# The second attention moved into the first phase, V in token order, and whole rows in the mixing by U

## The chip, the cores and the metric

The kernel runs on one core of one Trainium2 chip. The metric is the device time of one execution in microseconds (us), the time of the slowest core, here the only one. A run is told from another by about 0.3% of the time, some 2.6 us.

## The reference

Eight batches of eight heads: 32 packed queries `p` attend to 576 keys and values of width 64, and then 576 queries `q` attend to the 32 packed results. The heads are laid side by side (512 columns), tokens are mixed by a product of rank 32, and a two-layer network of 512, 2048 and 512 columns follows. `U`, `V`, `w_ch1` and `w_ch2` come as 64-bit floats, the rest as 32-bit.

```python
def sm_attn(qq, kk, vv):
    s = scale * np.matmul(qq, kk.transpose(0, 1, 3, 2))
    a = np.exp(s - np.max(s, axis=-1, keepdims=True))
    a = a / (np.sum(a, axis=-1, keepdims=True) + 1e-09)
    return np.matmul(a, vv)
p_packed = sm_attn(p, k, v)                # 8 x 8 x 32 x 64
x = sm_attn(q, p_packed, p_packed)         # 8 x 8 x 576 x 64, then 8 x 576 x 512
h = x.transpose(0, 2, 1) @ U @ V           # U 576 x 32, V 32 x 576
u = x + h.transpose(0, 2, 1)
out = u + np.maximum(u @ w_ch1, 0.0) @ w_ch2
```

## The kernel before

**Two phases.** In the first phase a planner reorders what the code records: it makes one fixed order for each engine from a timeline of its own, and each engine then runs its list strictly in that order. From `tc.manual_schedule()` on the code's own order stands.

**First phase.** The attention of `p` runs in 16 units, two groups `g` of four heads for each of eight batches. A unit loads keys (`a_load`, tile `kx`) and values (`a_load_v`, tile `vt`, three buffers), transposes the keys (`a_turn`, `kT`), forms scores (`a_scores`, `s_ps`), exponentials (`a_softmax`), turns them back (`a_turn_back`), multiplies by the values (`a_pack`, `two`) and transposes the packed result (`a_heads`, `ppT`; parked in DRAM as `ppTd` for later batches). Beside it w1 (16 chunks) and the first tiles of w2 are converted from 64-bit floats: ScalarE takes an absolute value (L77 or L143), VectorE makes four passes (L78 to L81, `float32_of`), and for w2 ScalarE and GpSimd split the result into a high and a low float32r part (L158, L159).

**The attention of `q`** is a list of 24 steps for one batch, made by `attention(b, res)`: `load` (two tiles `x` of 576 KB), three `turn_q` for each group, `scores_q`, four softmax steps (the exponents `e` have one buffer; max, subtraction on GpSimd, exp, sum, product on GpSimd, and transposition into `aT`), three `tokens` steps (back to token order, `x` tiles for the high and low part), `mix1` (ten products with U, L304) and four `mix2` (products with V, L318 and L321). Since the 32 packed rows replace keys and values, nothing is multiplied out here: `ah`/`al` hold mixed attention weights, and `fold` (L361) multiplies w1 by the packed rows. In V's tile `vs` the columns stand as the reference has them (token 9i + c), and `mix2` picks them with a stride of nine floats, since the other tiles keep the tokens in blocks of equal c.

Steps are popped one after the other. The code pops the first attention three steps to a unit from unit 4 on, and records the load of the second at unit 13:

```python
        if i >= 4:
            for _ in range(3):
                if first:
                    first.pop(0)()
```

**Second phase.** Eight steps, one to a batch, of 16 column blocks `kt`: `gemm1` (twelve products with `ah`, `al` into the two `h_ps` banks, then ScalarE's relu `hh` and VectorE's rest `hl`, L599), `gemm2` of the block before (twelve products of 512 columns into `o`), and after every fourth block (2, 6, 10, 14) a `fold` for the blocks to come, whose rest `wtl` VectorE forms (L368). In the first step the remaining w2 tiles are loaded and converted too, one to a block, and the last units' `a_pack` and `a_heads` run in its blocks 0 to 3. The attention steps of batch b + 1 are popped between these products in step b: in the first step that is the second attention. `bank()` gives one of two PSUM banks, shared by turns, scores, tokens, mixing and folds.

Line numbers are those of the profile of the kernel before; in the changed kernel they are up to 13 higher from L165 on.

Of the kernel before, what the change touches and what calls it, by code (L numbers as in the profile page):

```python
# [8 lines left out]
F32 = mybir.dt.float32  # L9
# [10 lines left out]
def packed_attention_mixer_kernel(  # L20
# [141 lines left out]

    ua4 = const.tile([P, 5, 4, R], F32R, name="ua4")
    vs = const.tile([P, S], F32R, name="vs")

    def x_tile():
        return pipe.tile([P, 5 * 2 * P], F32, name="x", tag="x", bufs=2)
# [12 lines left out]
    def prepare_uv(ub, vbits):  # L180
        ux = float32_of(conv_tile(I32)[:, :5 * R], conv_tile(F32)[:, :5 * R], ub.rearrange("p (x t) -> p x t", t=2))
        for (n, ks) in ((P, slice(0, 4)), (64, slice(4, 5))):
            nk = ks.stop - ks.start
            src = ux.rearrange("p (k r) -> p k r", k=5)[:n, ks].unsqueeze(2).to_broadcast([n, nk, 4, R])
            nc.vector.tensor_copy(ua4[:n, ks], src)
            nc.vector.tensor_tensor(ua4[:n, ks, 1], src[:, :, 0], ua4[:n, ks, 0].bitcast(F32), op=ALU.subtract)
        vb = vbits.rearrange("p (x t) -> p x t", t=2)
        n = I // 2
        for hf in range(2):
            cs = slice(NT * n * hf, NT * n * hf + NT * n)  # L190
            vx = float32_of(conv_tile(I32)[:, :NT * n], conv_tile(F32)[:, :NT * n], vb[:, cs])
            nc.vector.tensor_copy(vs[:, cs], vx)
            nc.vector.tensor_tensor(vs[96:, cs], vx[96:], vs[96:, cs].bitcast(F32), op=ALU.subtract)


    def load_nat(x, src, b, g):
        nc.sync.dma_start(
            out=x.rearrange("p (h y) -> p h y", h=2),
            in_=src[b, 4 * g:4 * g + 4].rearrange("(h z) (i c) d -> (z i) h (c d)", z=2, c=NT))

    def turn(t, x, h, bank):

        x = x.rearrange("p (h y) -> p h y", h=2)
        t_ps = bank()
        if h < 2:
            for j in range(4):
                o = P * (2 * (j % 2) + j // 2)
                nc.tensor.transpose(t_ps[:, o:o + P], x[:, h, P * j:P * j + P], ident)  # L208
            src = t_ps.rearrange("p (k a z i) -> p a z k i", k=2, a=2, z=2)
            for a in range(2):  # L210
                dst = t[:, 2 * h:2 * h + 2, :4 * I].rearrange("p z (k i a) -> p a z k i", k=2, a=2)[:, a]
                if a:
                    nc.vector.tensor_copy(dst, src[:, a])
                else:
                    nc.scalar.copy(dst, src[:, a])
        else:
            for h in range(2):
                nc.tensor.transpose(t_ps[:64, P * h:P * h + P], x[:, h, SM:], ident)
            nc.scalar.copy(t[:64, :, LAST], t_ps[:64, :2 * P].rearrange("p (h i) -> p h i", h=4))
# [21 lines left out]
    def attention(b, res):  # L241
# [43 lines left out]
        def tokens(k0):  # L285
            if k0 == 0:
                st["t"] = tuple(x_tile().bitcast(F32R).rearrange("p (k x) -> p k x", k=5) for x in "hl")
            th, tl = st["t"]
            t_ps = bank().rearrange("p (k x) -> p k x", k=2)
            n, rows = (2, P) if k0 < 4 else (1, I)  # L290
# [7 lines left out]
        def mix1():  # L298
            th, tl = st["t"]
            m_ps = bank()  # L300
            for kk in range(5):
                rows = P if kk < 4 else I
                for x, part in enumerate((th, tl)):
                    nc.tensor.matmul(m_ps[:, :2 * P], lhsT=ua4[:rows, kk], rhs=part[:rows, kk],  # L304
                                     start=kk == 0 and x == 0, stop=kk == 4 and x == 1)
            ms = st["ms"] = pipe.tile([P, 2 * P], F32R, name="ms", bufs=1)
            nc.scalar.copy(ms, m_ps[:, :2 * P])
# [3 lines left out]
        def mix2(g, hf):  # L311
            ah, al = res[b]
            aT = st["aT", g]
            ns = HALF[hf]
            v_ps = bank()[:, :ns.stop - ns.start]
            vc = vs.rearrange("p (i c) -> p c i", c=NT)
            lhsT = st["ms"][:, g * P:(g + 1) * P]
            nc.tensor.matmul(v_ps[:, :4 * I], lhsT=lhsT,  # L318
                             rhs=vc[:, hf:8 + hf:2].rearrange("p (a k) i -> p k i a", a=2), start=True, stop=True)
            if hf == 0:  # L320
                nc.tensor.matmul(v_ps[:, LAST], lhsT=lhsT, rhs=vc[:, 8], start=True, stop=True)  # L321
            nc.vector.tensor_tensor(aT[:, ns], v_ps, aT[:, ns], op=ALU.add)  # L322
            nc.scalar.copy(ah[:, g, ns], aT[:, ns])  # L323
            nc.gpsimd.tensor_tensor(al[:, g, ns], aT[:, ns], ah[:, g, ns].bitcast(F32), op=ALU.subtract)  # L324
# [159 lines left out]
    for n in range(4):  # L484
        load_w1(n)
    a_turn(0)
    first = attention(0, res)
    test_w1(0)

    def some_w1(n):  # L490
# [7 lines left out]
    for i in range(NU):  # L498
# [15 lines left out]
        if i > 2:  # L514
            a_heads(i - 3)
        if i >= 4:
            for _ in range(3):
                if first:
                    first.pop(0)()
        if i == 2:  # L520
# [5 lines left out]
            load_w2(1)  # L526
        if i == 13:
            fold(0, 0)
            steps = attention(1, res)
            steps.pop(0)()  # L530
        if i == 14:
            split_w2(*convert_w2(0))
            load_w2(2)
# [5 lines left out]
        lambda: (a_heads(NU - 1), tctx.close()),  # L539
    ]  # L540
    actx.close()


    ctx.enter_context(tc.manual_schedule())
# [116 lines left out]
            nc.sync.dma_start(out=out[b - 1 + i].rearrange("(i c) m -> c i m", c=NT)[8], in_=os_[I * i:I * i + I])  # L661

    w2x = convert_w2(1)
    last, parts = None, []
    for b in range(B):
        cur = Batch(b)
# [2 lines left out]
        for kt in range(NK):  # L669
# [2 lines left out]
                store_joint(b - 1, oj)  # L672
            if rest:
                rest.pop(0)()
            elif steps and (b == 0 or kt % 4 != 2):
                steps.pop(0)()
            if (b, kt) == (0, 5):
                w2_tiles(ctx.enter_context(tc.tile_pool(name="sC", bufs=1, side="right", reuse_waits="tile")), 2)
# [65 lines left out]
```

## Time and profile before

| What | us |
|---|---|
| median of three runs | 877.61 (877.48 to 879.47) |
| the profiled execution: its own time | 877.17 |
| its span, first to last instruction | 875.2 |
| TensorE busy in the span | 836.0 (96%) |
| VectorE, ScalarE, GpSimd busy | 402.6, 322.8, 95.0 |
| first product of `gemm1` (the seam of the phases) | at 122.36 |

The span is 2.0 us less than the time, and the difference lies outside the program. The profiled execution is 0.4 us under the median. Rows of the timeline give start, duration, engine, line, operation, output and inputs, and in brackets the idle time before the row with what ended it. Matmuls are pipelined, so the distance from one start to the next is what a product costs in a stream, and its own duration is longer. "SPq" is the queue on which the DMAs are issued, in order.

### The profile page before, as it was taken

How to read it: one execution, taken by the hardware profiler on the slowest of the kernel's cores; microseconds unless marked ns; L12 is line 12 of the kernel's file. 1: busy time of each engine (PE TensorE's matmuls, PEld its weight loads, DVE VectorE, ACT ScalarE, POOL GpSimd, SP SyncE). 2: the span in 40 equal slices, each digit the busy share in tenths (PEclk: the TensorE clock that was granted, in tenths of full speed). 3: DMA queues.
4: the chain of work that ended last, by engine and by line, in shares of the span. 5: the costliest groups of instructions: out<-in, count | busy, mean ns of one | idle time of the engine just before them, and what ended most of it. 6: DMA issues, size and time to landing. Idle time of an engine off the chain costs nothing.

```text
span 875.2 us, 14665 instructions
## 1 busy us (share of the span) xinstructions
PE 836.0 (96%) x5808; PEld 665.1 (76%) x5808; DVE 402.6 (46%) x988; ACT 322.8 (37%) x1000; POOL 95.0 (11%) x111
## 2 busy tenths in 40 slices
PE   5878899979999999999999999999999999999997
PEld 2554557858888888788878878888888887888886
DVE  4699757876433323433443433434343334332221
ACT  3666564534322333234223332233223332332221
POOL 0002222323001100100010000110011001010000
PEclk8799799989999999999999999999999999999999
DMA  8999833322100110011001100011001100010001
GB/s 273 290 337 292 278 115 102 95 75 85 49 1 1 61 53 10 1 61 49 1 1 61 49 13 1 1 61 49 1 1 61 48 13 1 1 49 1 1 1 60
DMA packets 38979, 59.08 MB, mean 68 GB/s; under 512 B 11776, under 2 KB 21888, under 8 KB 38912
## 3 DMA queue, kind: packets, MB, share of 16 engines
q1 hardware_dynamic: 38912, 58.16, 20.4%
q8 instruction: 45, 0.74, 0.4%
q14 instruction: 22, 0.18, 0.1%
HBM read 47.79 MB, written 10.35 MB: 66 GB/s over the span
## 4 chain that ended last, share of the span: by engine, by line
PE 85%; DVE 7%; DMA 4%; issue 1%; ACT 1%; POOL 0%; SPq 0%; ACTq 0%; DVEq 0%; POOLq 0%
PE o L86 16%; PE o L88 16%; PE o L87 16%; PE h_ps L86 8%; PE h_ps L88 7%; PE h_ps L87 7%; PE t_ps L361 4%; DMA bits<-in_moe_w_ch_dram 2%; PE t_ps L208 1%; DVE os L80 1%; PE t_ps L229 1%; PE s_ps L229 1%; PE t_ps L304 1%; PE t_ps L236 1%; DMA x<-in_moe_U_dram 1%
## 5 line engine op out<-in xcount | busy, mean ns | idle before, releaser
L86 PE MATMUL o<-w2h,hh 128*128 128x512 f32 x512 | 208.7, 408 | 0.0
L88 PE MATMUL o<-w2h,hl 128*128 128x512 f32 x512 | 203.5, 397 | 0.0
L87 PE MATMUL o<-w2l,hh 128*128 128x512 f32 x512 | 203.0, 397 | 0.0
L599 DVE SCALAR_TENSOR_TENSOR hl<-h_ps,hh 128x256 fp32r<-128x256 f32 x256 | 104.4, 422 | 167.2 <-ACT hj L598 154.4
L596 ACT ACTIVATE hh<-h_ps 128x256 fp32r<-128x256 f32 x256 | 98.9, 388 | 188.9 <-PE h_ps L88 188.1
L86 PE MATMUL h_ps<-ah,wth 128*128 128x320 f32 (+1 forms) x512 | 158.2, 309 | 1.2 <-DVE hl L599 1.2
L87 PE MATMUL h_ps<-al,wth 128*128 128x320 f32 (+1 forms) x512 | 151.6, 296 | 0.0
L88 PE MATMUL h_ps<-ah,wtl 128*128 128x320 f32 (+1 forms) x512 | 151.4, 296 | 0.0
L86 PEld LDWEIGHTS h_ps<-ah,wth 128*128 128x128 f32 x512 | 96.9, 189 | 32.7 <-issue 25.7
L88 PEld LDWEIGHTS o<-w2h,hl 128*128 128x128 f32 x512 | 97.1, 190 | 23.1
L86 PEld LDWEIGHTS o<-w2h,hh 128*128 128x128 f32 x512 | 97.4, 190 | 22.2 <-issue 4.1
L87 PEld LDWEIGHTS o<-w2l,hh 128*128 128x128 f32 x512 | 97.6, 191 | 17.4
L87 PEld LDWEIGHTS h_ps<-al,wth 128*128 128x128 f32 x512 | 97.0, 189 | 1.9
L88 PEld LDWEIGHTS h_ps<-ah,wtl 128*128 128x128 f32 x512 | 97.0, 190 | 0.0
L368 DVE TENSOR_TENSOR wtl<-t_ps,wth 128x256 fp32r<-128x256 f32 x128 | 48.5, 419 | 93.9 <-ACT wth L367 90.5
L367 ACT CAST wth<-t_ps 128x256 fp32r<-128x256 f32 x128 | 43.4, 374 | 109.1 <-PE t_ps L361 97.1
L324 POOL TENSOR_TENSOR al<-aT,ah 128x320 fp32r<-128x320 f32 (+1 forms) x32 | 26.2, 818 | 211.6 <-ACT ah L323 211.6
L268 POOL TENSOR_TENSOR e<-e,m 128x576 f32<-128x576 f32 x16 | 19.6, 1226 | 237.8 <-DVE m L267 232.4
L361 PE MATMUL t_ps<-w1t,ppT 64*32 64x512 f32 x512 | 36.5, 601 | 0.0
L323 ACT CAST ah<-aT 128x320 fp32r<-128x320 f32 (+1 forms) x32 | 13.9, 433 | 52.8 <-DVE aT L322 52.8
L279 POOL TENSOR_TENSOR e<-e,s 128x576 f32<-128x576 f32 x16 | 18.9, 1179 | 110.3 <-DVE s L278 106.4
L296 DVE TENSOR_TENSOR x<-t_ps,x 128x512 fp32r<-128x512 f32 (+1 forms) x24 | 14.3, 599 | 32.6 <-ACT x L295 32.6
(130 smaller groups left out, 1021.9 us busy)
## 6 DMA issues: line engine op xcount, KB each, us to landing
bits<-in_moe_w_ch_dram SPq DMA_DIRECT2D x32, 512.0 KB, 4.9
kx<-in_k_dram SPq DMA_DIRECT2D x16, 576.0 KB, 6.1
x<-in_q_dram SPq DMA_DIRECT2D x16, 576.0 KB, 4.8
vt<-in_v_dram SPq DMA_DIRECT2D x64, 128.0 KB, 4.9
out_dram<-bits SPq DMA_DIRECT2D x32, 256.0 KB, 2.4
pn<-in_p_dram SPq DMA_DIRECT2D x16, 64.0 KB, 5.6
vt<-in_v_dram SPq DMA_DIRECT2D x16, 64.0 KB, 4.2
out_dram<-os SPq DMA_DIRECT2D x8, 128.0 KB, 2.3
```

Source lines behind the costliest of these rows:

```text
L86: nc.tensor.matmul(ps, lhsT=lh, rhs=rh, start=start, stop=False)
L87: nc.tensor.matmul(ps, lhsT=lh, rhs=rl, start=False, stop=False)
L88: nc.tensor.matmul(ps, lhsT=ll, rhs=rh, start=False, stop=stop)
L229: nc.tensor.matmul(ss[r][hs, :n], lhsT=lT[rs, g, hs], rhs=t[rs, h, :n], start=True, stop=True)
L268: nc.gpsimd.tensor_tensor(e, e, m.unsqueeze(2).to_broadcast([P, S // 32, 32]), op=ALU.subtract)
L279: nc.gpsimd.tensor_tensor(e, e, s.unsqueeze(2).to_broadcast([P, S // 32, 32]), op=ALU.mult)
L324: nc.gpsimd.tensor_tensor(al[:, g, ns], aT[:, ns], ah[:, g, ns].bitcast(F32), op=ALU.subtract)
L361: nc.tensor.matmul(f_ps[g][xs], lhsT=ppT[b][zs, g, xs], rhs=w1t[h // 2][zs, QW * c:QW * c + QW], start=True, stop=True)
L367: nc.scalar.copy(hi[:, g], f_ps[g][:, cs])
L368: nc.vector.tensor_tensor(lo[:, g], f_ps[g][:, cs], hi[:, g].bitcast(F32), op=ALU.subtract)
L596: nc.scalar.activation(hh[:, ms], src, AF.Relu)
L599: nc.vector.scalar_tensor_tensor(hl[:, ms], src, 0.0, hh[:, ms].bitcast(F32), op0=ALU.max, op1=ALU.subtract)
```

## The change

Five edits, in one step:

- The list `first` holds both attentions, 48 steps, and four are popped for each unit from 4 on: 4 x 12 = 48, so none is left for the first step of the second phase. The second attention's load is recorded at unit 10 where it was 13.
- V's columns are stored in the order of the blocks, in `prepare_uv`: three pieces for each half of V where there was one. `mix2` then needs one product over a contiguous slice.
- The fifth block of U and of the token tiles has 64 rows; the other 64 are set to zero on GpSimd, and `mix1` multiplies all 128 rows.
- In the second phase both halves of a turned tile are copied by ScalarE (`split_copies`), where VectorE took one.
- The condition for popping in the first step is now that of all steps.

```diff
+    nc.gpsimd.memset(ua4[I:, 4].bitcast(F32), 0.0)
...
-            nc.vector.tensor_copy(vs[:, cs], vx)
-            nc.vector.tensor_tensor(vs[96:, cs], vx[96:], vs[96:, cs].bitcast(F32), op=ALU.subtract)
+            vx = vx.rearrange("p (i c) -> p i c", c=NT)
+            blocks = vx[:, :, :8].rearrange("p i (a k r) -> p r k i a", a=2, k=2)
+            ns = slice(n * hf, n * hf + n)
+            pairs = [(vs[:, LAST][:, ns], vx[:, :, 8])]
+            for r in range(2):
+                dst = vs[:, HALF[r].start:HALF[r].start + 4 * I].rearrange("p (k i a) -> p k i a", k=2, a=2)[:, :, ns]
+                pairs.append((dst, blocks[:, r]))
+            for dst, src in pairs:
+                nc.vector.tensor_copy(dst, src)
+                nc.vector.tensor_tensor(dst[96:], src[96:], dst[96:].bitcast(F32), op=ALU.subtract)
...
-                if a:
+                if a and split_copies:
                     nc.vector.tensor_copy(dst, src[:, a])
...
+                for t in st["t"]:
+                    nc.gpsimd.memset(t[I:, 4].bitcast(F32), 0.0)
...
-                rows = P if kk < 4 else I
-                    nc.tensor.matmul(m_ps[:, :2 * P], lhsT=ua4[:rows, kk], rhs=part[:rows, kk],
+                    nc.tensor.matmul(m_ps[:, :2 * P], lhsT=ua4[:, kk], rhs=part[:, kk],
...
-            nc.tensor.matmul(v_ps[:, :4 * I], lhsT=lhsT,
-                             rhs=vc[:, hf:8 + hf:2].rearrange("p (a k) i -> p k i a", a=2), start=True, stop=True)
-            if hf == 0:
-                nc.tensor.matmul(v_ps[:, LAST], lhsT=lhsT, rhs=vc[:, 8], start=True, stop=True)
+            nc.tensor.matmul(v_ps, lhsT=st["ms"][:, g * P:(g + 1) * P], rhs=vs[:, ns], start=True, stop=True)
...
-    first = attention(0, res)
+    first = attention(0, res) + attention(1, res)
...
-            for _ in range(3):
+            for _ in range(4):
...
-            steps = attention(1, res)
-            steps.pop(0)()
...
+    split_copies = False
...
-            elif steps and (b == 0 or kt % 4 != 2):
+            elif steps and kt % 4 != 2:
```

Since a planner orders the first phase, the built programs are shown at three places. First SP's queue around the second attention's loads (`x` from `in_q`; `kx` and `vt` are keys and values, `bits` are w2's tiles). Before:

```order
L197 DMA kx_1533<-in_k_dram 128x2x576
L151 DMA bits_1576<-in_moe_w_ch2_dram 128x1024
L403 DMA vt_1266<-in_v_dram 128x1x256 x4
L404 DMA vt_1266<-in_v_dram 64x4x64
L151 DMA bits_1578<-in_moe_w_ch2_dram 128x1024
L197 DMA kx_1635<-in_k_dram 128x2x576
L403 DMA vt_1389<-in_v_dram 128x1x256 x3
L479 DMA ppTd3_75<-ppTa_1221 128x256
L403 DMA vt_1389<-in_v_dram 128x1x256
L404 DMA vt_1389<-in_v_dram 64x4x64
L197 DMA x_1695<-in_q_dram 128x2x576
L197 DMA x_1697<-in_q_dram 128x2x576
```

The same place now:

```order
L206 DMA kx_1599<-in_k_dram 128x2x576
L206 DMA x_1391<-in_q_dram 128x2x576
L206 DMA x_1393<-in_q_dram 128x2x576
L400 DMA pn_1596<-in_p_dram 128x2x64
L410 DMA vt_1318<-in_v_dram 128x1x256 x4
L411 DMA vt_1318<-in_v_dram 64x4x64
L400 DMA pn_1596<-in_p_dram 128x2x64
L151 DMA bits_1668<-in_moe_w_ch2_dram 128x1024
L206 DMA kx_1725<-in_k_dram 128x2x576
```

The two loads of `q` moved ahead of the values of unit 11, of w2's second tile and of the last keys.

Second, TensorE's list at the seam (`s_ps` are the scores of the last unit, `aT` the second attention's transposed weights, `h_ps` the first `gemm1`). Before:

```order
L229 MATMUL s_ps_1810<-kT_1730,pT_1610 32x256 x4
L238 MATMUL m_ps_1803<-ident_66,e1_1754 64x128
L473 MATMUL t_ps_1852<-ident_66,two_1778 128x128
L463 MATMUL m_ps_1827<-vt_1505,eT_1701 32x64 x20
L86 MATMUL h_ps0_1894<-ah_1358,wth_1683 128x320
L87 MATMUL h_ps0_1894<-al_1359,wth_1683 128x320
```

And now:

```order
L240 MATMUL s_ps_1944<-kT_1825,pT_1700 32x256 x4
L470 MATMUL m_ps_1961<-vt_1571,eT_1796 32x64 x20
L480 MATMUL t_ps_1876<-ident_66,two_1756 128x128
L247 MATMUL t_ps_1884<-ident_66,aT0_1651 128x128
L247 MATMUL t_ps_1891<-ident_66,aT0_1651 128x128
L247 MATMUL t_ps_1884<-ident_66,aT1_1772 128x128
L247 MATMUL t_ps_1884<-ident_66,aT0_1651 128x128
L247 MATMUL t_ps_1884<-ident_66,aT1_1772 128x128
L247 MATMUL t_ps_1891<-ident_66,aT1_1772 128x128
L247 MATMUL t_ps_1891<-ident_66,aT0_1651 128x128
L247 MATMUL t_ps_1891<-ident_66,aT1_1772 128x128
L86 MATMUL h_ps0_2048<-ah_1164,wth_1784 128x320
```

Eight of the second attention's ten `tokens` products now stand ahead of the first `gemm1`, and need both groups' `aT`; the last two, `mix1` and the four `mix2` stand right behind it.

Third, VectorE's list in the first step's blocks 9 and 10, around the third fold (`wtl`). Before:

```order
L278 RECIPROCAL s_2570<-s_2570 128x18
L599 SCALAR_TENSOR_TENSOR hl_2576<-h_ps0_2577,hh_2575 128x256
L599 SCALAR_TENSOR_TENSOR hl_2576<-h_ps1_2587,hh_2575 128x256
L283 STREAM_TRANSPOSE aT1_2596<-e_2486 128x576
L78 TENSOR_SCALAR os_2615<-os_2615 128x512
L79 TENSOR_SCALAR os_2614<-os_2615 128x512
L80 SCALAR_TENSOR_TENSOR os_2614<-bits_2561,os_2614 128x512
L81 SCALAR_TENSOR_TENSOR os_2614<-bits_2561,os_2614 128x512
L368 TENSOR_TENSOR wtl_2632<-t_ps_2621,wth_2631 128x256
L368 TENSOR_TENSOR wtl_2632<-t_ps_2622,wth_2631 128x256
```

And now:

```order
L605 SCALAR_TENSOR_TENSOR hl_2646<-h_ps0_2647,hh_2645 128x256
L605 SCALAR_TENSOR_TENSOR hl_2646<-h_ps1_2657,hh_2645 128x256
L78 TENSOR_SCALAR os_2683<-os_2683 128x512
L79 TENSOR_SCALAR os_2682<-os_2683 128x512
L80 SCALAR_TENSOR_TENSOR os_2682<-bits_2636,os_2682 128x512
L81 SCALAR_TENSOR_TENSOR os_2682<-bits_2636,os_2682 128x512
L375 TENSOR_TENSOR wtl_2700<-t_ps_2689,wth_2699 128x256
L375 TENSOR_TENSOR wtl_2700<-t_ps_2690,wth_2699 128x256
```

The softmax of the second attention (`s`, `aT1`) has left this place.

More of the change, by code (lines that the diff above doesn't have):

```diff
@@ L199, in load_nat @@
             in_=src[b, 4 * g:4 * g + 4].rearrange("(h z) (i c) d -> (z i) h (c d)", z=2, c=NT))
+    split_copies = True
     def turn(t, x, h, bank):
@@ L315, in mix2 @@
             v_ps = bank()[:, :ns.stop - ns.start]
-            vc = vs.rearrange("p (i c) -> p c i", c=NT)
-            lhsT = st["ms"][:, g * P:(g + 1) * P]
-            nc.tensor.matmul(v_ps[:, :4 * I], lhsT=lhsT,
-                             rhs=vc[:, hf:8 + hf:2].rearrange("p (a k) i -> p k i a", a=2), start=True, stop=True)
-            if hf == 0:
-                nc.tensor.matmul(v_ps[:, LAST], lhsT=lhsT, rhs=vc[:, 8], start=True, stop=True)
+            nc.tensor.matmul(v_ps, lhsT=st["ms"][:, g * P:(g + 1) * P], rhs=vs[:, ns], start=True, stop=True)
             nc.vector.tensor_tensor(aT[:, ns], v_ps, aT[:, ns], op=ALU.add)
@@ L663, in packed_attention_mixer_kernel @@
     w2x = convert_w2(1)
+    steps = []
     last, parts = None, []
```

## The prediction

> **What bounds the kernel now.** I first split the span at the seam of the phases (the first `gemm1` at 122.36) and at the folds of block 2, which stand once in each step, in the view of busy times by stretch. Its columns are the stretch, its length, busy us and instructions of each engine, the granted TensorE clock, and the DMA engines' share and rate.
>
> ```profile
> 90.00:107.00 17.00, 13.77 (x163) 9.19 (x159) 12.43 (x26) 9.27 (x27) 3.62 (x4) 0.80 0.91 287
> 107.00:122.36 15.36, 15.21 (x219) 8.33 (x219) 8.72 (x30) 10.29 (x35) 5.18 (x12) 0.86 0.47 141
> 122.36:138.16 15.80, 14.52 (x162) 12.12 (x156) 11.42 (x29) 10.86 (x37) 5.14 (x8) 1.00 0.42 132
> 138.16:234.60 96.44, 90.79 (x578) 73.62 (x584) 66.78 (x135) 41.18 (x116) 23.44 (x20) 0.96 0.25 81
> 333.99:420.85 86.86, 86.58 (x559) 70.95 (x564) 34.30 (x85) 28.65 (x91) 7.86 (x8) 1.00 0.08 28
> ```
>
> The third step (333.99 on) is what a step costs undisturbed: TensorE is busy 86.58 of 86.86 at full clock. The same stretch of the first step takes 96.44, and there the busy time and the clock both have holes. Up to 107 the DMA engines are 0.91 busy and VectorE 12.43 of 17.00; after that neither is full, and TensorE's 15.21 of 15.36 at clock 0.86 is made of short products, whose modelled ends overlap. So the kernel is bound by TensorE from the seam on, and ahead of it by loads, then by chains between engines. Work taken off TensorE in the second phase counts in full; work put into the first counts by what it delays at the seam.
>
> Next the holes of the first step, from its timeline (TensorE, then VectorE, then one stretch of TensorE alone):
>
> ```profile
> 184.78 0.41 PE L86 MATMUL h_ps<-ah,wth 128*128 128x320 f32 x1 [1.23 <-DVE hl L599]
> 186.23 0.28 PE L87 MATMUL h_ps<-al,wth 128*128 128x256 f32 x1
> 186.35 0.28 PE L88 MATMUL h_ps<-ah,wtl 128*128 128x256 f32 x1
> 190.46 1.08 PE L236 MATMUL t_ps<-ident,aT 128*128 128x128 f32 x4 [3.83 <-DVE wtl L368]
> ...
> 196.47 0.62 PE L236 MATMUL t_ps<-ident,aT 128*128 128x128 f32 x4
> ...
> 185.72 0.78 DVE L283 STREAM_TRANSPOSE aT<-e 128x576 f32<-128x576 f32 x1 [0.67 <-POOL e L279]
> ...
> 189.04 1.28 DVE L368 TENSOR_TENSOR wtl<-t_ps,wth 128x256 fp32r<-128x256 f32 x3
> ...
> 192.00:194.00 2.00, 2.00 (x6) 0.50 0.06 25
> ```
>
> TensorE waits 1.23 for `hl` at 184.78 and 3.83 at 190.46. The second wait is for a PSUM bank: the token products of the second attention need one that the third fold still holds, VectorE empties it only at 189.04, and it is late since it had first waited for the softmax's product (0.67 before L283) and then had a w2 tile to convert. After that pause the clock stands at 0.50, and it is back when the products at 196.47 are through; 190.46 to 196.47 at half clock cost 3.0. In all 1.23 + 3.83 + 3.0 = 8.1.
>
> **What the first step saves.** The last step holds no attention, so the distance of two of its folds is four bare blocks, from the chain of work that ended last:
>
> ```profile
> 813.07 1.02 PE t_ps L361 x16
> 831.87 1.02 PE t_ps L361 x16
> ```
>
> 18.80 for four blocks with their fold. A bare step is 4 x 18.80, and 24 products of the residual at 0.12 each (the distance from 186.23 to 186.35), 2.9: 78.1. One attention therefore costs 86.86 - 78.1 = 8.8 on TensorE, handovers included. From its first fold to the next step's the first step will hold no attention of its own, only the first four steps of the next one, about 2.0 (4 of 23 steps would be 1.5, and a score step is one of the longer): 80.1 instead of 96.44, a gain of 16.3. The parts of the 96.44 agree: 78.1, 2.0, 8.8 less the two turns ahead of the first fold (0.8), and the holes 8.1 make 96.2. I take 16; 9 if only the products go and the holes come back elsewhere, 17 at most.
>
> The head of the first step, 122.36 to 138.16, loses the two turns (0.8) and gains what the order put behind the first `gemm1`: two token products, `mix1` and the four `mix2`. These stand in steady steps so (TensorE's timeline in the second step):
>
> ```profile
> 285.89 1.54 PE L304 MATMUL t_ps<-x,ua 128*128 128x256 f32 x10
> 287.36 0.50 PE L86 MATMUL o<-w2h,hh 128*128 128x512 f32 x1
> ...
> 290.27 0.39 PE L318 MATMUL t_ps<-vs,ms 128*128 128x256 f32 x1
> ...
> 290.54 0.38 PE L86 MATMUL h_ps<-ah,wth 128*128 128x320 f32 x1
> ...
> 295.37 0.39 PE L318 MATMUL t_ps<-vs,ms 128*128 128x256 f32 x1
> 295.58 0.33 PE L86 MATMUL h_ps<-ah,wth 128*128 128x320 f32 x1
> ```
>
> `mix1` takes 1.47 (285.89 to 287.36), two `mix2` 0.27 each and two 0.21, now some 0.6 in all (below), the two token products 0.1: 2.2 more. Nothing covers their waits: they follow each other at once, `mix1`'s end needs the last token piece, which VectorE makes behind both `hl`; `mix2` needs ScalarE's and VectorE's `ms`; the third and fourth `mix2` need a bank that VectorE must empty. Queued behind them on TensorE are the last units' `a_pack` and the second `gemm1`, and on SP the fourth w2 tile behind the store of `ppTa`. The nearest row for such a wait is 1.85, before the first attention's last `mix2`:
>
> ```profile
> 107.14 0.58 PE L318 MATMUL t_ps<-vs,ms 128*128 128x256 f32 x1 [1.85 <-DVE aT L322]
> ```
>
> Between none and three of these (0 to 5.6) I take 3.0, less 0.6 of the 1.28 idle that the head has already (15.80 - 14.52). Head: -0.8 + 2.2 + 3.0 - 0.6, about +4, from +1 to +6.
>
> **What the mixing saves.** A contiguous 256-column product takes 0.12 in the stream, the strided one of V 0.21, and strided 256 with the 64 columns behind them 0.27. In token order 320 columns take 0.15 (0.12 x 320/256) and 256 take 0.12. Per attention 2 x 0.12 + 2 x 0.09 = 0.4. U's ten products take 1.47 where ten of 0.12 take 1.2; whole rows can recover at most 0.27, and I take 0.1. Six attentions lie in the TensorE-bound steps 1 to 6: 6 x 0.5 = 3, from 1 (only the 64-column products go) to 4. The zeros are memsets on GpSimd (busy 7.86 of 86.86 there), the pieces of V a few more VectorE instructions near 45 us; hidden by that idle time and by the loads, and at worst 1 us at the seam. The turns' second half adds four copies to ScalarE per attention:
>
> ```profile
> L215 ACT COPY xT<-t_ps 128x256 f32<-128x256 f32 x24 | 9.4, 390 | 36.0 <-PE t_ps L208 35.4
> ```
>
> 1.6 us beside 28.65 busy of 86.86, covered by products; without that cover the next `gemm1` would wait for `hh`, and at most 6 x 1.6 would show. I cost it at nothing.
>
> **What the first phase pays.** Rows around the seam (SP's queue, ScalarE, VectorE, TensorE):
>
> ```profile
> 93.86 0.54 SPq L151 DMA_DIRECT2D bits<-in_moe_w_ch_dram  x1
> 101.47 1.85 SPq L197 DMA_DIRECT2D x<-in_q_dram  x2
> ...
> 101.42 0.66 ACT L77 ACTIVATE os<-bits 128x512 f32<-128x512 f32 x1 [1.06 <-DMA bits<-in_moe_w_ch_dram]
> ...
> 60.12 0.51 DVE L261 STREAM_TRANSPOSE e<-t_ps 128x320 f32<-128x320 f32 x1
> 60.55 0.41 DVE L262 STREAM_TRANSPOSE e<-t_ps 128x256 f32<-128x256 f32 x1
> ...
> 88.39 0.77 DVE L283 STREAM_TRANSPOSE aT<-e 128x576 f32<-128x576 f32 x1
> ...
> 105.89 0.81 DVE L433 TENSOR_REDUCE mx<-s_ps 128x1 f32<-128x320 f32 x2
> ...
> 99.57 0.38 PE L304 MATMUL t_ps<-x,ua 64*128 64x256 f32 x1
> ...
> 122.36 0.42 PE L86 MATMUL h_ps<-ah,wth 128*128 128x320 f32 x1
> ```
>
> The first attention now gets its steps sooner; its `mix1`, which ended near 100 (99.57), stands two units earlier, which I put at 92 to 93. The loads of `q` wait for that (same `x` buffers), and are issued there instead of at 101.47. w2's second tile is now behind them: issued at 93.86 it reached ScalarE at 101.42, and 2 x 576 KB at 287 GB/s are 4.1 more, so 101.4 to 105.5. VectorE and ScalarE run in order, so the maxima of unit 12 (105.89) wait for that tile's conversion: 106 to 110, say 108. Between these maxima stands the transposition of the second attention's first scores, and from there a chain runs to the eight token products ahead of the first `gemm1`, twice in series since `e` has one buffer:
>
> ```profile
> L267 DVE TENSOR_REDUCE m<-e 128x18 f32<-128x576 f32 x12 | 9.0, 747 | 0.2
> L268 POOL TENSOR_TENSOR e<-e,m 128x576 f32<-128x576 f32 x12 | 13.9, 1160 | 218.6 <-DVE m L267 218.6
> L271 ACT ACTIVATE e<-e 128x576 f32<-128x576 f32 x12 | 8.2, 683 | 0.0
> L276 DVE TENSOR_REDUCE s<-e 128x18 f32<-128x576 f32 x12 | 9.0, 748 | 0.9
> L279 POOL TENSOR_TENSOR e<-e,s 128x576 f32<-128x576 f32 x12 | 13.9, 1161 | 95.6 <-DVE s L278 95.6
> L283 DVE STREAM_TRANSPOSE aT<-e 128x576 f32<-128x576 f32 x12 | 9.3, 773 | 8.0 <-POOL e L279 8.0
> ```
>
> 0.51 + 0.41 for the transpositions at 60, then 0.75, 1.16, 0.68, 0.75, 1.16, 0.77: 6.2 for a group, 12.4 for both with nothing between. With VectorE full the first attention took from 60.12 to the end of L283 at 89.2, 29.1. From 90 to the seam VectorE was busy 12.43 + 8.72 of 32.36 and gets some 10 more (the passes above, turns and tokens), so it will be neither free nor full all along; the units' passes stand between those of the chain, one unit's round of exponentials between each pair of them. I take the middle, 20.5, and 0.5 for the token products: the first `gemm1` at 108 + 21 = 129, or 6.6 later. A clock below full in the looser end adds 1: 7.5. From below, TensorE alone gets two score steps, a turned group and eight token products more ahead of the seam, 8 of 23 steps or 3. From above, 110 + 29.1 + 0.5 = 139.6 gives 17.
>
> **Sum**, against the execution's own 877.17: first phase +7.5, head +4, rest of the first step -16, mixing -3: -7.5, so 869.7, which I call 870. The median of the runs before is 0.4 higher, within their scatter.
>
> **Rivals.**
> *The chain at the seam decides (slower).* If the second softmax runs as slowly as the first did, the first product comes at 139.6, and TensorE, idle before it, starts at half clock, 3.0 by the hole at 190: 17 + 3 instead of 7.5 gives 882. It decides from a first product at about 137 on (7.2 later than forecast). For it: the 29.1 is the only softmax in the first phase that the trace shows. Against it: that one ran beside the w1 conversions, which are over by then.
> *The seam hides nearly all.* The chain fits into the units' own waits and only TensorE's 3 shows: 865.
> *The clock falls at the seam.* If TensorE waits long for the second `aT`, the first `gemm1` and the mixing run at half clock. By the row at 190, 3.83 of idling was enough and 6.0 of work were needed to come back: 3.0 more, 873. The Trainium skill (TensorE: Matmul & The Clock Gate, section "What's actually happening") says that the clock halves after an idle window of about 3.4 us and returns after about 3.4 us of sustained work; by that the price would be 1.7 and the sum 871. The 3.83 agrees with its first half, the 6.0 is longer than its second.
> *The w2 tiles take over the first step.* With TensorE at 4.70 a block (18.80 / 4) a tile must come as often.
>
> ```profile
> bits<-in_moe_w_ch_dram SPq DMA_DIRECT2D x32, 512.0 KB, 4.9
> ```
>
> Load 4.9, ScalarE 0.66, VectorE about 2.5 (from the end of L283 at 186.5 to 189.04) make 8.1 for one of two buffers, 4.1 a block. That is 0.6 below 4.70; loads 2.2 slower would make it 5.2, and 16 x 0.5 = 8 would come back: 878, no change.
> *The mixing gains nothing,* because the products with V are slow for another reason than the stride: 873.
>
> **How the numbers follow.** Forecast 45%, hidden seam 15%, clock 12%, mixing without gain 5% (all faster by over 0.3%, that is below 874.5), w2 tiles 11% (within 0.3%), slow chain 12%. The forecast's own upper edge loses a little to "same": faster 75%, same 13%, slower 12%. The range 862 to 881 leaves out the best bounds together and the far end of the slow chain.
>
> **What the profile will show.** Right: the first `gemm1` between 126 and 132, no wait over 1 us between the folds of the first step and full clock there, about 80 between its first fold and the next step's; the third step near 86.4; products with V at the duration of other contiguous ones. Wrong: a first product after 137, or a wait of ScalarE's L77 for `bits` in each block of the first step. I would be most wrong in the 20.5 of the chain, whose ends are 12.4 and 29.1.

## The result, and the profile after

| | before | changed |
|---|---|---|
| median (lowest to highest of 6 runs) | 879.05 (877.48 to 882.04) | 872.38 (870.57 to 874.37) |
| ratio to before, 95% interval | | 0.9921 [0.9899, 0.9942] |
| profiled execution: time, span, mean clock | 877.17, 875.2, 0.973 | 874.37, 872.6, 0.967 |

The change makes the kernel 6.7 us faster; the forecast was 870. Medians here and below are of the fast executions: three slow ones, of 1014.5, 1321.0 and 1942.4 us, are left out. The profiled execution of the changed kernel is the slowest of its six. Between the two profiled executions only 2.8 us remain, and their sum has to be read with that in mind.

The stretches of the changed kernel that answer to those of before, in the view of busy times by stretch (same columns): ahead of the first `gemm1`, the head, the rest of the first step, a whole step later on, and ten microseconds of the first phase.

```profile
60.00:133.65 73.65, 61.28 (x770) 37.61 (x769) 57.74 (x152) 45.04 (x139) 20.98 (x28) 0.81 0.73 233
133.65:153.21 19.56, 17.66 (x166) 14.49 (x164) 13.74 (x29) 12.22 (x38) 9.31 (x16) 0.94 0.21 65
153.21:237.85 84.64, 82.00 (x508) 67.54 (x514) 56.67 (x115) 36.21 (x104) 16.03 (x13) 0.98 0.31 98
336.30:422.22 85.92, 85.65 (x556) 70.36 (x562) 32.64 (x81) 29.67 (x95) 8.42 (x10) 1.00 0.08 28
100.00:110.00 10.00, 9.80 (x85) 6.08 (x85) 4.50 (x15) 6.24 (x21) 3.14 (x6) 0.56 0.59 199
```

The first `gemm1` starts at 133.65 instead of 122.36 (+11.3). The head takes 19.56 instead of 15.80 (+3.8), the rest of the first step 84.64 instead of 96.44 (-11.8), a later step 85.92 instead of 86.86 (-0.94). From the next step's first fold to the end it is 874.37 - 237.85 = 636.5 against 877.17 - 234.60 = 642.6 (-6.1). 11.3 + 3.8 - 11.8 - 6.1 = -2.8, the difference of the two executions.

Where the first step still loses time, TensorE's timeline of the changed kernel, and VectorE's beside it:

```profile
153.21 1.09 PE L368 MATMUL t_ps<-w1t,ppT 64*32 64x512 f32 x16
154.86 0.41 PE L86 MATMUL h_ps<-ah,wth 128*128 128x320 f32 x1 [0.56 <-DVE hl L605]
...
158.80 0.30 PE L480 MATMUL t_ps<-ident,two 128*128 128x128 f32 x1 [2.08 <-DVE wtl L375]
...
159.41 0.39 PE L88 MATMUL o<-w2h,hl 128*128 128x512 f32 x1
...
161.52 0.63 PE L88 MATMUL o<-w2h,hl 128*128 128x512 f32 x1
...
163.40 0.28 PE L87 MATMUL o<-rdl,ah 128*128 128x256 f32 x1
...
154.39 0.75 DVE L605 SCALAR_TENSOR_TENSOR hl<-h_ps,hh 128x256 fp32r<-128x256 f32 x2
155.05 0.42 DVE L78 TENSOR_SCALAR os<-os 128x512 f32<-128x512 f32 x1
...
157.37 1.61 DVE L375 TENSOR_TENSOR wtl<-t_ps,wth 128x256 fp32r<-128x256 f32 x4
```

The hole of before (3.83 at 190.46) is gone, since no token product stands behind a fold any more. Another takes part of its place: the last unit's heads (L480) are transposed in the block behind the first fold and ask for a PSUM bank that the fold still holds; VectorE empties it late, because a w2 tile's conversion (155.05 to 157.37) stands ahead of L375. After the 2.08 of waiting the products of 512 columns take 0.63 instead of 0.39, from about 159.9 to 163.2.

The mixing in the second step, TensorE's timeline of the changed kernel (the rows of before, from 285.89 on, are in the prediction):

```profile
289.14 1.35 PE L316 MATMUL t_ps<-x,ua 128*128 128x256 f32 x10
290.33 0.39 PE L86 MATMUL o<-w2h,hh 128*128 128x512 f32 x1
...
293.15 0.31 PE L328 MATMUL t_ps<-vs,ms 128*128 128x320 f32 x1
293.29 0.32 PE L86 MATMUL h_ps<-ah,wth 128*128 128x320 f32 x1
...
297.85 0.28 PE L328 MATMUL t_ps<-vs,ms 128*128 128x256 f32 x1
297.97 0.31 PE L86 MATMUL h_ps<-ah,wth 128*128 128x320 f32 x1
```

From its start to the next product, `mix1` takes 1.19 (before 1.47), the first `mix2` 0.14 (0.27), one without the last column 0.12 (0.21). Contiguous and whole operands run as other products of their width do. The first product behind each is shorter too: 0.39 for 0.50 behind `mix1`, 0.32 for 0.38 behind `mix2`.

### The profile page after: what moved, and what is told of

The parts are those of the page before. It is cut to its first block, busy times and chain, and to the rows that moved or that the text cites. A ratio compares the mean times of both kernels' runs of the same rounds, so it can differ in the third digit from the quotient of the medians.

```text
span 872.6 us, 14704 instructions
## 1 busy us (share of the span) xinstructions
PE 831.3 (95%) x5792; PEld 664.3 (76%) x5792; DVE 393.1 (45%) x972; ACT 329.0 (38%) x1024; POOL 100.1 (11%) x128
## 4 chain that ended last, share of the span: by engine, by line
PE 86%; DVE 6%; DMA 3%; ACT 1%; SPq 1%; issue 1%; POOL 0%; ACTq 0%; DVEq 0%; POOLq 0%
PE o L86 16%; PE o L88 16%; PE o L87 16%; PE h_ps L86 8%; PE h_ps L87 8%; PE h_ps L88 8%; PE t_ps L368 4%; PE t_ps L219 2%; DMA bits<-in_moe_w_ch_dram 1%; PE t_ps L240 1%; PE t_ps L316 1%; PE s_ps L240 1%; PE t_ps L247 1%; DVE os L80 1%; DMA vt<-in_v_dram 1%; DMA x<-in_moe_U_dram 1%
## 5 line engine op out<-in xcount | busy, mean ns | idle before, releaser
L86 PE MATMUL o<-w2h,hh 128*128 128x512 f32 x512 | 206.3, 403 | 0.0
L375 DVE TENSOR_TENSOR wtl<-t_ps,wth 128x256 fp32r<-128x256 f32 x128 | 48.4, 419 | 94.5 <-ACT wth L374 91.2
L226 ACT COPY xT<-t_ps 128x256 f32<-128x256 f32 x56 | 19.2, 391 | 39.4 <-PE t_ps L219 38.0
L219 PE MATMUL k_ps<-ident,kx 128*128 128x128 f32 x128 | 24.0, 338 | 5.7 <-DMA kx<-in_k_dram 4.9
```

What stands on the lines that cost most here:

```text
L86: nc.tensor.matmul(ps, lhsT=lh, rhs=rh, start=start, stop=False)
L375: nc.vector.tensor_tensor(lo[:, g], f_ps[g][:, cs], hi[:, g].bitcast(F32), op=ALU.subtract)
```

## The experiments

One table for all of them. "First gemm1", "first fold" and "next fold" are the starts, in the profiled execution, of the first `gemm1`, of the first fold behind it, and of the first fold of the next step; "behind it" is the execution's time less the next fold. Each ratio is to executions of the kernel before that ran beside the experiment (their medians are 879.05 to 880.24).

| kernel | median | ratio to before, 95% interval | first gemm1 | first fold | next fold | behind it |
|---|---|---|---|---|---|---|
| before | 879.05 | | 122.36 | 138.16 | 234.60 | 642.6 |
| changed | 872.38 | 0.9921 [0.9899, 0.9942] | 133.65 | 153.21 | 237.85 | 636.5 |
| move only | 876.07 | 0.9964 [0.9943, 0.9986] | 133.24 | 153.24 | 237.84 | 643.0 |
| V's order only | 872.31 | 0.9919 [0.9891, 0.9948] | 123.12 | 139.02 | 234.98 | 638.7 |
| mixing only (V and U) | 868.61 | 0.9873 [0.9850, 0.9896] | 121.26 | 137.38 | 232.19 | 636.5 |
| changed, copies shared | 871.74 | 0.9918 [0.9886, 0.9950] | 129.74 | 149.09 | 231.78 | 636.6 |
| 16 of 24 steps moved | 875.38 | 0.9947 [0.9924, 0.9970] | 134.34 | 150.95 | 240.94 | 636.5 |
| 11 of 24 steps moved | 878.53 | 1.0001 [0.9984, 1.0018] | 134.70 | 153.88 | 245.62 | 636.8 |
| one unit earlier | 871.15 | 0.9905 [0.9882, 0.9929] | 138.54 | 153.89 | 238.54 | 636.5 |
| heads a block later | 868.90 | 0.9884 [0.9864, 0.9903] | 132.97 | 151.70 | 232.49 | 636.5 |
| mixing only, no step at folds | 870.13 | 0.9887 [0.9865, 0.9909] | 121.41 | 140.62 | 234.04 | 637.2 |
| heads later, copies on ScalarE | 866.06 | 0.9834 [0.9807, 0.9862] | 129.21 | 149.14 | 229.88 | 636.5 |
| mixing only, copies on ScalarE | 868.71 | 0.9881 [0.9860, 0.9902] | 119.75 | 135.44 | 230.26 | 636.5 |
| the fastest, one unit earlier | 868.63 | 0.9872 [0.9853, 0.9891] | 134.86 | 150.21 | 231.00 | 636.5 |

The last column is the first finding. With the new mixing ten of eleven kernels need 636.5 to 636.8 behind the next step's first fold, whatever stands ahead; with the old mixing 642.6 and 643.0. So a kernel's time is settled by that fold, and what differs from kernel to kernel lies ahead of it.

### The two halves of the change

The mixing without the move (its attention steps as before, the copies shared throughout):

```
-    first = attention(0, res) + attention(1, res)    -> attention(0, res), 3 steps a unit
-    steps = []                                       -> attention(1, res) from i == 13 on
```

> The kernel before with V in token order and whole rows of U, the second attention still in the first step. Theory A (the steady steps of the two profiles: 86.86 to 85.92 us a step, 5.7 us over the steps from the second on): the mixing carries most of the gain; 7 attentions in the second phase at 0.8 to 0.95 make -5.5 to -6.6 us, ratio 0.9925 to 0.994, and a third step of 85.9. Theory B (the prediction's price, 0.5 an attention): -3 to -3.5 us, ratio 0.996, and a third step of 86.4.

The move alone, with V and U as before:

```
-    first = attention(0, res)
+    first = attention(0, res) + attention(1, res)    (4 steps a unit, no steps in the first step)
```

> The kernel before with only the move: both attentions in the first phase, V and U as before. Theory A (seam 11 later, head 4 longer, rest of the first step 12 to 16 shorter): between +3 and -1.5 us, ratio 0.998 to 1.003, the third step at 86.9. Theory B (the prediction's terms, 7.5 + 4 - 16): -4.5 us, ratio 0.995, with the first gemm1 near 129.

V's order without U's whole rows (the mixing-only kernel with `ua4[:rows, kk]` and `part[:rows, kk]` again, without the zeros):

> As the mixing-only kernel, but U's last 64 rows multiplied as 64 rows again (no zeros), so only V's order is new. Theory A (V's stride carries it, as the prediction has it, 0.4 of 0.5): 0.7 to 0.9 of the mixing-only gain, third step at most 0.3 us longer than with whole rows. Rival (the 64-row products carry it, 1.47 to 1.19 us for the ten products of a mixing): about 0.3 us per attention, 2 us in 7 attentions, is lost against the mixing-only kernel, so that it gains some 3.5 to 4.5.

The length of a step stands in the chain of work that ended last, as the distance of the folds of one block; move only, V's order only, mixing only:

```profile
337.26 1.02 PE t_ps L361 x16
424.11 1.02 PE t_ps L361 x16
```

```profile
333.80 1.02 PE t_ps L366 x16
420.07 1.02 PE t_ps L366 x16
```

```profile
330.64 1.02 PE t_ps L368 x16
416.54 1.02 PE t_ps L368 x16
```

86.85, 86.27 and 85.90, where before has 86.86 and the changed kernel 85.92. The move does nothing to a later step. V's order takes off 0.59, whole rows 0.37, and both do so in every step: behind the next fold 642.6 becomes 638.7 with V and 636.5 with U as well. So 3.9 us are V's and 2.2 are U's. For the mixing theory A has the step right (85.9) and B is too small. For V alone the rival's price is the nearer one (0.37 a step and 2.2 us lost without whole rows, forecast 0.3 and 2), though V still carries 0.6 of the gain in a step. The whole gain of V's order, 7.2 us in medians, is 0.66 of the mixing's, a little under theory A's 0.7 to 0.9 and well over the rival's 3.5 to 4.5 us.

The mixing alone is worth 10.9 us in medians (879.55 beside it, 868.61), more than the whole change (theory A said 5.5 to 6.6). The profiled executions differ by 8.5: 6.1 behind the next fold, 1.6 in the rest of the first step (137.38 to 232.19 is 94.81), 1.1 ahead of the first `gemm1`, less 0.3 in the head. The medians add 2.4, since the profiled execution of before lies that much below its median. Why the first phase is a little shorter is not settled. In the 1.6 lie the second attention's own mixing, 0.96, and a shorter half clock behind the hole, 3.41 us where the kernel before has 6.83 (first row: before; second: mixing only). The kernel before is idle in the first 0.8 of its 6.83, so about 1.3 of the 3.0 that the prediction gave to this half clock are not in the mixing-only execution. With the 0.96 this would make 2.3; where the rest was lost again is not settled.

```profile
189.68:196.51 6.83, 6.05 (x17) 4.80 (x18) 5.13 (x10) 2.88 (x8) 1.28 (x1) 0.50 0.22 77
```

```profile
190.21:193.62 3.41, 3.41 (x11) 2.64 (x10) 2.50 (x5) 1.69 (x3) 1.28 (x1) 0.50 0.29 115
```

The move alone gains 3.5 in medians, inside neither theory's narrow range but nearer to B, though its profiled execution (880.81, among the slowest of its runs) shows A's: seam +10.9, head +4.2, rest -11.8. Added to the mixing the same move loses: 868.61 to 872.38. Its balance is a small difference of large terms. Why it gains on the old mixing and loses on the new, 7 us apart in medians, is not shown. In the changed kernel as it stands, the move is not where the gain comes from.

### The copies on ScalarE

```
 split_copies = True
 ...
-    split_copies = False
```

(the line behind the first phase is left out)

> The changed kernel, but with the turned x copies still shared between VectorE and ScalarE in the second phase (before: half on each). Theory A (the prediction: the four copies more on ScalarE are covered by products): the time of the changed kernel within 1 us (872), steps within 0.1 us. Rival (VectorE, busy 71 of 87 in a step, is what the copies hold up, and part of the 0.94 us gained per step is theirs): 0.2 to 0.5 us per step is lost, 1.5 to 3 us in all, 874 to 875.

The medians are 0.6 apart with overlapping intervals, and the steps 85.90 and 85.92: the copies cost nothing. The run shows something else as well. Its instructions on TensorE are those of the changed kernel in the same order, and its first phase is written alike, so it shows the same first phase a second time; the kernel with later heads (below) shows it a third time:

```profile
60.00:129.74 69.74, 55.57 (x784) 33.10 (x773) 58.32 (x155) 44.22 (x137) 20.27 (x27) 0.93 0.77 245
```

```profile
60.00:132.97 72.97, 60.44 (x773) 37.03 (x773) 58.35 (x153) 44.56 (x137) 19.09 (x26) 0.84 0.74 233
```

Clock 0.93, 0.84 and (changed kernel, above) 0.81 go with a first `gemm1` at 129.74, 132.97 and 133.65, at the same VectorE time of 58. For most of these 4 us it is not shown whether the lower clock makes TensorE late or a TensorE that waits more lowers the clock. For one part it is shown. From the second attention's first scores (`t_ps<-xT,ppT`, at 112.59 in the changed kernel) to the first `gemm1` the three do the same work in the same order. The first two rows are the changed kernel, the third the one with later heads:

```profile
112.59:133.65 21.06, 18.00 (x272) 9.93 (x263) 15.97 (x46) 13.55 (x46) 6.88 (x12) 0.89 0.40 108
129.19:136.02 6.83, 6.69 (x66) 5.15 (x65) 3.25 (x8) 3.66 (x12) 3.77 (x10) 0.50 0.08 23
```

```profile
113.67:132.97 19.30, 16.13 (x272) 8.78 (x263) 15.86 (x46) 12.87 (x44) 6.21 (x10) 1.00 0.39 107
```

With shared copies it is 19.30 too (110.44 to 129.74). So 1.8 us of the changed kernel's seam are the half clock of that one execution, and the rest of the difference lies ahead of this stretch.

### What sets the seam

The second attention's steps, cut after the softmax of the second group or of the first; the others are taken in the first step again:

```
-    first = attention(0, res) + attention(1, res)
+    second = attention(1, res)
+    first = attention(0, res) + second[:16]          (or [:11])
 ...
-    steps = []
+    steps = second[16:]                              (or [11:])
```

> The changed kernel, but only the first 16 of the second attention's 24 steps (through its last softmax step) in the first phase; its token products and mixing are taken in the first step of the second phase. Theory S1 (a chain ends last: the first gemm1 waits for the second group's softmax and the token products): the first gemm1 comes 5 to 7 us earlier, the head loses 3, the rest of the first step gains 3 for the mixing: -5 to -7 against the changed kernel, 865 to 867. Theory S2 (TensorE's and VectorE's work ahead of the seam at a low clock ends last, the chain would be covered): only the token products, 2.3 us at half clock, go: 869.5 to 871.

> As the last, but only the first 11 steps (through the first group's softmax) in the first phase. S1: the whole second softmax leaves the path to the first gemm1, seam 7 to 9 us earlier than in the changed kernel, near 125, the rest 3 to 4 longer: 865 to 868. S2: two score steps and their share of VectorE leave the first phase, seam 3 to 4 earlier: 869 to 871, and a new wait at a fold if one of the later steps meets it.

Stretches from the second attention's first scores to the first `gemm1`, and behind the first fold, 16 steps and then 11:

```profile
116.34:134.34 18.00, 15.15 (x265) 8.04 (x256) 15.52 (x45) 11.76 (x39) 5.51 (x7) 1.00 0.43 113
...
150.95:240.94 89.99, 85.96 (x524) 70.56 (x531) 57.66 (x115) 38.00 (x110) 18.65 (x16) 0.96 0.26 87
```

```profile
118.06:134.70 16.64, 16.13 (x249) 7.96 (x240) 12.60 (x39) 11.54 (x40) 5.76 (x12) 1.00 0.43 114
...
153.88:245.62 91.74, 85.12 (x532) 69.11 (x538) 63.26 (x128) 39.86 (x113) 20.48 (x19) 1.00 0.26 85
```

Theory S1 falls. With 16 steps TensorE's list up to the first `gemm1` is the changed kernel's without the eight token products. Without them the stretch takes 18.00 where it takes 19.30 at full clock, and without the second softmax too 16.64: 1.3 and 2.7 us less, where S1 had 5 to 7 and 7 to 9. What is left of it with 11 steps is nearly full of TensorE's own short products (16.13 of 16.64). The seam itself stands no earlier, at 134.34 and 134.70, since these executions reach the stretch later (116.34 and 118.06, the others 110.44 to 113.67); with 16 steps TensorE's and VectorE's lists up to there are those of the changed kernel, so for that kernel this is scatter of the first phase. S2 is nearer but was too hopeful as well: it forecast a gain, and both medians are above the changed kernel's (with 16 steps the intervals overlap), since the steps put back open new holes in the first step (with 11 steps TensorE idles 91.74 - 85.12 = 6.6, against 2.6 in the changed kernel).

```
-        if i >= 4:
+        if i >= 3:        (behind load_uv and prepare_uv, 4 steps a unit)
```

> The changed kernel with both attentions' steps starting one unit earlier (from unit 3), four a unit. S1: all of the chain stands a unit, some 6 us, earlier; the seam moves by 4 to 6: 866 to 868. S2: VectorE was full from 70 to 90 and gets the work still earlier; seam within 1.5 of the changed kernel's: 871 to 874.

The first `gemm1` comes at 138.54, with `mix1` and the first `mix2` now ahead of it, and the first fold at 153.89 instead of 153.21, in the slowest of the six executions: no gain shows. The median (871.15) is 1.2 lower, within the intervals and within S2's range; S2's seam (within 1.5 of the changed kernel's) was not met, as more products stand ahead of it.

### The hole behind the first fold

```
         lambda: (a_pack(NU - 1, bank), a_heads(NU - 2)),
+        lambda: None,
         lambda: (a_heads(NU - 1), tctx.close()),
```

> The changed kernel with the transposition of the last unit's heads taken one block later, in the block behind the fold's, so that it doesn't ask for the PSUM bank which the fold still holds. Theory A (the wait of 2.08 us at 158.80 and the half clock behind it cost 3 to 4 us): first fold to the next step's first fold near 81 instead of 84.5, 868 to 869.5. Rival (VectorE's conversion of the w2 tile is late anyway and the next product for it waits as long): within 1 us of the changed kernel, 872.

```profile
132.97:151.70 18.73, 16.69 (x168) 13.36 (x166) 13.54 (x29) 12.60 (x40) 9.99 (x17) 1.00 0.26 78
151.70:232.49 80.79, 80.23 (x508) 66.37 (x513) 56.68 (x115) 36.13 (x104) 16.03 (x13) 1.00 0.31 102
```

Theory A: the stretch takes 80.79 at full clock, 3.85 less than in the changed kernel, and the median falls by 3.5 to 868.90. With the hole closed the first step is worth what the prediction priced it at.

The same was tried the other way round, on the mixing-only kernel, which still has the hole of before:

```profile
189.75 0.66 PE L247 MATMUL t_ps<-ident,aT 128*128 128x128 f32 x4 [3.89 <-DVE wtl L375]
190.13 0.70 PE L86 MATMUL o<-w2h,hh 128*128 128x512 f32 x1
...
193.61 0.41 PE L88 MATMUL o<-w2h,hl 128*128 128x512 f32 x1
```

```
-            elif steps and (b == 0 or kt % 4 != 2):
+            elif steps and kt % 4 != 2:              (and the first group's three turns in the first phase)
```

> The mixing-only kernel (second attention still in the first step), but no attention step is taken in the three blocks of the first step that hold a fold, as in all later steps; the three steps that this leaves over, the first group's turns, go into the first phase instead. Theory A (the wait of 3.9 us for the fold's bank, the half clock behind it, 1.7, and the 1.2 for hl are all that the move could win in the first step beyond shifting work): -4 to -6 against the mixing-only kernel, 863 to 865, less than 1 us later at the seam. Rival (the pause moves to the next step that asks for a bank, or the three turns delay the seam as the whole attention does): 867 to 870.

The rival is nearer: 870.13, with the first `gemm1` at 121.41, so the wait moved and the seam did not. TensorE's waits from its first `gemm1` to the next fold are now several smaller ones:

```profile
PE t_ps L247 <- DVE e L272: 2.0, 1, 2.0
PE t_ps L240 <- DVE wtl L375: 1.9, 1, 1.9
PE t_ps L480 <- DVE wtl L375: 1.1, 1, 1.1
PE t_ps L247 <- DVE aT L294: 1.1, 1, 1.1
```

### VectorE in the first phase

The kernel with later heads, and `split_copies = False` from the start, so that ScalarE makes all copies of turned q and k:

> The changed kernel with the heads one block later, and all the copies of turned q and k on ScalarE in the first phase too, which takes some 10 us of copies from VectorE between 60 us and the seam (57 busy of 73) and gives them to ScalarE (45 of 73). Theory V (VectorE, full from 58 to 100, delays the units and lets TensorE's clock fall): seam 3 to 6 us earlier than the 133 to 134 of the kernels with both attentions there, 863 to 866. Rival (loads, or TensorE's own short products, set the units' pace, or ScalarE becomes the next bound): within 1.5 of 868.9, or later.

```profile
60.00:129.21 69.21, 57.20 (x763) 35.04 (x758) 48.67 (x126) 48.19 (x157) 19.26 (x28) 0.85 0.78 249
129.21:149.14 19.93, 17.76 (x167) 14.60 (x165) 13.72 (x29) 12.20 (x38) 9.11 (x16) 0.94 0.21 65
149.14:229.88 80.74, 80.18 (x508) 66.35 (x514) 56.63 (x115) 36.13 (x104) 16.02 (x13) 1.00 0.31 102
```

VectorE's time ahead of the seam falls from 58.35 to 48.67, the first `gemm1` comes 3.8 earlier at the same clock (0.85 and 0.84), the first fold 2.6, and the median is 866.06, 2.8 lower. The seam alone would not show it, since the same first phase scatters as much; the medians do, as every execution (861.89 to 866.39) is faster than every one of the kernel with later heads alone (867.24 to 870.95). Theory V holds, at the weak end of its ranges, except that a rise of the clock does not show. This is the fastest of all: 0.9834 of before, against 0.9921.

> The mixing-only kernel (no move) with the first phase's copies of turned q and k all on ScalarE; the second phase shares them as before. Theory A (the copies relieve VectorE whether the second attention is there or not): 2 to 4 us below the mixing-only kernel's 868.6, 865 to 866.5, so that the move is worth nothing beside it. Theory B (VectorE is only too full where two attentions stand in the first phase): within 1 us of 868.6, and the move is worth 2 to 3 once VectorE is relieved.

The same copies without the move give 868.71 where it was 868.61: theory B. Only with two attentions in the first phase do the copies on VectorE cost anything in the median. With the heads later and the copies on ScalarE the move is worth 868.71 - 866.06 = 2.6 us, though the two intervals still touch.

> The fastest kernel so far (both attentions in the first phase, heads one block later, first-phase copies on ScalarE, 866.06) with the attentions' steps starting one unit earlier. Theory A (with VectorE relieved the end of the two softmaxes and of the mixing is late by itself, so a unit earlier helps): 862 to 864.5. Rival (TensorE's short products fill the last units, so nothing is won, as with the changed kernel, where an earlier start gave 1.2): 865 to 866.5.

868.63, slower than either expectation (ratio 0.9872 [0.9853, 0.9891] against 0.9834 [0.9807, 0.9862]; the intervals overlap a little). Even with VectorE relieved an earlier start doesn't pay; the first fold comes at 150.21 instead of 149.14. What holds the first phase of the fastest kernel, with no engine full from 60 to the seam (TensorE 57 of 69, VectorE and ScalarE 48 to 49 each), was not found.

## Why the prediction was right, term by term, and where it was not

**First phase, +7.5: right in size by an estimate, from misses of opposite sign.** The profiled execution shows 11.3, but it is the slowest of its runs. Taking each kernel's time behind the first `gemm1` as fixed (877.17 - 122.36 = 754.8 and 874.37 - 133.65 = 740.7), the medians put that product at 124.2 and 131.7, which is +7.4 (an estimate; it leans on the constant last column of the table). The steps to it failed in two places. The rows are VectorE's, ScalarE's and TensorE's:

```profile
110.07 0.68 ACT L77 ACTIVATE os<-bits 128x512 f32<-128x512 f32 x1
...
113.13 0.48 DVE L440 TENSOR_REDUCE mx<-s_ps 128x1 f32<-128x320 f32 x1
...
130.49 0.77 DVE L294 STREAM_TRANSPOSE aT<-e 128x576 f32<-128x576 f32 x1
...
131.68 2.32 PE L247 MATMUL t_ps<-ident,aT 128*128 128x128 f32 x8
133.65 0.62 PE L86 MATMUL h_ps<-ah,wth 128*128 128x320 f32 x1
```

Unit 12's maxima came at 113.13, not 108 (at 110.97 and 114.20 in the other two executions of this first phase), and not because w2's second tile landed late: L77 shows no wait for `bits`. In the ten microseconds before, TensorE was busy 9.80 at clock 0.56 and VectorE only 4.50. From there the two softmaxes took 18.1 (to 131.26), not 20.5. And this chain, which the step took for what places the seam, places only its last part: the seam gains 2.7 us when the second softmax and the token products are taken out. At full clock the way from unit 12's maxima to the first `gemm1` is 18.8 in both other executions, and 16.5 before (105.89 to 122.36), so it adds 2.3; the larger part of the term is lost ahead of those maxima, where the step had 2.1. What delays them was not isolated. The added work of TensorE and VectorE, with a clock that differs between executions, is the likely cause; that the copies on VectorE take part in it is shown.

**Head, +4: measured +3.8**, but made otherwise. TensorE's idle time in the head grew from 1.28 to 1.90, by 0.6 where the sum had 3.0 - 0.6 = 2.4. The half clock, which lasted to 136.02, gave about 1.2 (half of the 2.37 from 133.65 on), and that the term had left out.

**Rest of the first step, -16: measured -11.8.** The step that failed is "holes 8.1 go". 1.23 + 3.83 + 3.0 went, but 2.08 and some 1.7 of half clock (half of 3.4) came at 158.80, at a product that I had not followed: the last unit's heads, which asked for the bank of the first fold instead of the third's. With that repaired the stretch is 80.79, where the working said 80.1. So the sign of no wait over 1 us and full clock between these folds did not come in the changed kernel.

**Mixing, -3: measured -6.1** behind the next fold, 0.96 instead of 0.5 per step. Both parts were undersized. V was put at 0.4 and gives 0.59: the products themselves save 0.40, the other 0.2 lie in the product behind each, which is shorter too. U was put at 0.1 of at most 0.27 and gives 0.37: all of that bound (1.47 to 1.19) and 0.1 in the product behind.

**ScalarE's copies, 0: confirmed** by the run with shared copies.

So the sum came out near (-7.5 forecast, -6.7 measured) because the mixing gave 3 more and the first step 4 less. That these two misses cancel is luck.

**The rivals.** The slow chain (from 137 on) did not come, nor did the w2 tiles, whose conversions show no wait for `bits` in the first step. The seam did not hide the move, and the mixing gained. A falling clock was there in part: the token products at 131.68 and the first `gemm1` ran at half speed in the profiled execution (0.62 for the 0.39 that the run with shared copies shows), but no long wait for `aT` preceded it. The Trainium skill (TensorE: Matmul & The Clock Gate, section "What's actually happening") has the clock come back after about 3.4 us of sustained work; the half clock from 159.91 to 163.33 agrees with it, and so does that of before, which the prediction took for longer: TensorE was idle at the start of the first of its two stretches of 3.41 us (189.68 to 190.46) and busy all through the second. It has the clock fall after an idle window of about 3.4; here TensorE was still busy 1.33 of the 3.41 us ahead of the fall at 159.91.

## What to carry to other kernels

When a stage is bound by one engine, price every operand that it reads with a stride or in part rows by the product behind it as well; such a saving repeats in each step and adds up, while work moved into an earlier phase can pay there nearly what it saves. Before forecasting that a wait disappears, list every other product that asks for the same bank in the same blocks: the next one in line inherits the wait. And judge a moved stage by medians and by a point from which the rest is constant, since a single execution's first phase can differ by 4 us or more from the next.

## What the runs showed of the hardware

- A whole-row product can be cheaper than a part-row one: ten products of 256 columns, two of them with 64 rows, took 1.47 us; the same ten with 128 rows 1.19. The price lies where the number of rows changes too: the whole-row product just ahead of the two, and the two themselves, take 0.21, 0.22 and 0.21 to the next start, where whole rows take 0.12.
- A strided operand also lengthens the next product's record: 0.38 against 0.32 for the 320 columns behind the first `mix2`, 0.33 against 0.31 behind one without the last column.
- The half clock does not start with the wait: after the 2.08 us the first products still took 0.39 (at 159.41), and 0.63 only from about 160. The clock stood at 1.00 or 0.50 and changed only on a grid of 3.41 us in all fourteen traces. Every such 3.41 us at full clock in which TensorE was busy under 0.48 of the time was followed by half clock, and none in which it was busy over 0.86. In the changed kernel:

```profile
156.50:159.91 3.41, 1.33 (x8) 0.98 (x8) 3.07 (x8) 2.09 (x8) 0.00 (x0) 1.00 0.00 0
159.91:163.33 3.42, 3.42 (x10) 2.65 (x9) 2.63 (x4) 0.58 (x2) 1.28 (x1) 0.50 0.62 192
```

- The same first phase (one of the four lacks two memsets on GpSimd) reached the second attention's first scores at 110.44, 112.59, 113.67 and 116.34 us in four executions. The granted clock from 60 us to that row was 0.90, 0.77, 0.78 and 0.79.
